# An attention and SoLU kernel: pair sums ahead of the block means, one transfer on another queue, and tiles at multiples of 512 bytes

## The chip, the cores and the metric

The kernel runs on one core of a Trainium2 chip. The metric is the device time of one execution in microseconds (us), the median over the runs shown; lower is better. The core's engines are TensorE (PE in the profile, with its weight loads as PEld), VectorE (DVE), ScalarE (ACT), GpSimd (POOL) and SyncE (SP, which here only issues transfers). Each has its own instruction stream and works through it in order; they wait for each other by semaphores. SBUF is the on-chip memory, 128 partitions wide; PSUM is where TensorE writes.

## The reference

Four batches of eight heads, 768 positions, head dimension 64. Each query sees the 31 keys around it and, besides, 24 summaries: every block of 32 keys is summarised by the maximum of its keys and by the mean of its values.

```python
k_sum = k.reshape(B, H, nb, block, D).max(axis=3)
v_sum = v.reshape(B, H, nb, block, D).mean(axis=3)      # the "means" below
scores_l = scale * np.matmul(q, k.transpose(0, 1, 3, 2))     # masked to |i - j| < 16
scores_s = scale * np.einsum('bhsd,bhnd->bhsn', q, k_sum) + np.log(block)
...
a = softmax over both together
x = np.matmul(a, np.concatenate([v, v_sum], axis=2))
...
h = x @ w_in                        # 512 -> 1024
solu = h * softmax(h)
ln = layernorm(solu) * g_ln
out = ln @ w_out                    # 1024 -> 512
```

`x` is rearranged to 3072 rows of 512 before `w_in`. Inputs and outputs are fp32.

## The kernel before

**Work and order.** The 3072 rows are 24 row blocks of 128 (t = 0 to 23). A group (b, g) is batch b and four windows of 64 queries (g = 0, 1, 2); it makes two row blocks. For each half of a group `scores` (line 578) forms the scores of four heads, VectorE adds the mask (597), ScalarE takes the exponentials (605), `values_turn` transposes them (633), and `values` (664, 672) multiplies with the values. The result goes to `xh` and `xl`, a rounded high part and the rest. `first(t)` (697) makes `h` from them in two halves of 512 columns; after the SoLU and its normalisation `turn(t)` transposes (633) into `lh` and `ll`, and `second(t)` (775) makes `o` and sends it out. Each product with `w_in` or `w_out` is three matmuls of 128 x 512 (high by low, low by high, high by high), the stationary operand a 128 x 128 piece of `xh`, `xl`, `lh` or `ll`, the moving one half of a `w` tile. So a row block of `h` is 2 x 4 x 3 = 24 matmuls, and one of `o` is 8 x 3 = 24 (the last is halved, 48 in two column halves).

**Weights.** `load_w` brings 16 raw tiles of 512 KB, and `rounded`, `split_w_in` and `split_w_out` turn each in place into a high and a low half, with some seven instructions on ScalarE and VectorE, sometimes GpSimd. These fill VectorE and ScalarE in the first 100 us.

**The means.** `vsum` is one tile, with the 24 means of a batch in partitions 96 to 119. For batch 0, `load_v_rows` (447) loads all values in three `st_v` tiles of two times 128 rows of 512 (each 512 KB), and `mean_values_first` (459) multiplies them with a selector: `sel` holds 1/32 where a row belongs to a block. That is six fp32 matmuls into one bank; the profile shows each as two entries. For batch 1 `mean_values_pe` (472) does it with another layout and selector (`sel_q`), and four small transfers on ScalarE's queue (485) put the rows into `vsum`. Batches 2 and 3 add on GpSimd (501) instead. `load_v2` (541) copies the means from `vsum` into the `vt` tile of a group, beneath its window values. For (0, 1) and (0, 2) this transfer is issued by ScalarE, for batches 1 to 3 by SyncE. Group (0, 0) has none: it multiplies with `vsum` directly (664).

**The planner.** The order of all engines is written out by a planner at build time. An `op` names the engines that can take it with a cost for each (`ADD_W = ((dve, 0.62), (pool, 1.46))`), the tiles it reads and writes, and from these its dependences. An operation's due time is the least position in the list among TensorE operations that need it. `order` simulates: each engine takes the ready operation that can begin first, then the one due first, but leaves an operation to another engine that would end it earlier. `issue` does that 64 times, 63 of them with noise on the due times, and keeps the order with the earliest planned end of TensorE. Where TensorE has to wait in the first 80 us, `keep_up` puts in fillers: bf16 matmuls of zeros (line 900), into a bank that is free.

**Where tiles lie.** A tile gets its address when it is first used, so small and large ones lie mixed. The `w` tiles follow `ident`, `mhalf`, `mask`, `g_sb` and `zero`. Of the tiles below, the remainder of the address by 512 is, in the program as built:

| tile | buffer 0 | buffer 1 | used by |
|---|---|---|---|
| all `w` tiles (4096 bytes) | 96 | | moving operand of 697 and 775 |
| `xh` and `xl` | 160 | 32 | 697; a group uses buffer (3b + g) mod 2 |
| `lh` | 160 | 352 | 775; buffer t mod 2 |
| `ll` | 352 | 96 | 775; buffer t mod 2 |

A 128 x 128 piece starts at a multiple of 512 bytes within its tile, a half of `w` at a multiple of 2048.

**Queues.** SyncE's order of first loads is the string `LOADS` (w for weights, k, q, r for `st_v`, v); its transfers share one queue. `load_v2` waits for the `load_v` of its group and for `vsum`; line 485 may write `vsum` only when every earlier `load_v2` has read it.

Of the kernel before, what the change touches and what calls it, by code (L numbers as in the profile page):

```python
# [11 lines left out]
F32 = mybir.dt.float32  # L12
F32R = mybir.dt.float32r
BF16 = mybir.dt.bfloat16
# [3 lines left out]
ALU = mybir.AluOpType  # L18
AX = mybir.AxisListType

P = 128
B, H, S, D = 4, 8, 768, 64
BLOCK, WINDOW = 32, 16
NB = S // BLOCK
DM, DF = H * D, 1024
# [7 lines left out]
WIN = QT + 2 * HALO  # L33
KC = WIN + NB
# [17 lines left out]
class Buf:  # L52


    def __init__(self, make, prev=()):
        self.make, self.prev, self.tile = make, prev, None
        self.ops, self.writers, self.readers, self.gone = [], {}, {}, False
# [15 lines left out]
class Plan:  # L73
# [14 lines left out]
    TRIES, NOISE = 64, 3.0  # L88

    def __init__(self):  # L90
        self.ops, self.rings, self.banks, self.idle = [], {}, {}, None

    def buf(self, pool, shape, dtype, tag, bufs, name):
        ring = self.rings.setdefault(tag, [])
        slot = f"{tag}_{len(ring) % bufs}"
        b = Buf(lambda: pool.tile(shape, dtype, tag=slot, bufs=1, name=name), ring[-bufs:][:1] if len(ring) >= bufs else ())
        ring.append(b)
        return b

    def place(self, make, bank, tag):  # L100

        b = Buf(make, [self.banks[bank]] if bank in self.banks else ())
        self.banks[bank] = b
        self.rings.setdefault(tag, []).append(b)
        return b

    def op(self, engine, cost, fn, r=(), w=(), nbytes=0, after=(), alt=(), port=False):

        deps = set(after)

        def of(table, part):
            for k, v in table.items():
                if part is None or k is None or k == part:
                    deps.update(v)

        o = Op({e: (c, f) for e, c, f in ((engine, cost, fn), *alt)}, deps,
               len(self.ops), nbytes, port)
        r = [x if isinstance(x, tuple) else (x, None) for x in r]  # L120
        w = [x if isinstance(x, tuple) else (x, None) for x in w]
        for b, part in r:
            of(b.writers, part)
        for b, part in w:
            of(b.writers, part)
            of(b.readers, part)
            for p in b.prev:
                deps.update(p.ops)
                p.gone = True
        assert not any(b.gone for b, _ in r + w)  # L130
        for b, part in r:
            b.readers.setdefault(part, []).append(o)
            b.ops.append(o)
        for b, part in w:
            b.writers.setdefault(part, []).append(o)
            b.ops.append(o)
        deps.discard(o)
        self.ops.append(o)
        return o
# [115 lines left out]
def attn_then_solu(ctx: ExitStack, tc: tile.TileContext, q, k, v, vr, vb, w_in, w_out, g_ln, out):  # L255
# [3 lines left out]
    nc = tc.nc  # L259
    plan = Plan()  # L260
    op = plan.op
    pe, act, dve, pool, sp = "pe", "act", "dve", "pool", "sp"
# [6 lines left out]
    COPY_X = ((act, 0.48), (dve, 0.6))  # L269
    LO_W = ((dve, 0.6), (pool, 1.4))  # L270
    ADD_W = ((dve, 0.62), (pool, 1.46))
    MUL_E = ((pool, 1.8), (dve, 1.07))

    const = ctx.enter_context(tc.tile_pool(name="const", bufs=1))
    sb = ctx.enter_context(tc.tile_pool(name="sb", bufs=1))
# [11 lines left out]
    def tt(costs, kind, to, a, b, **k):  # L287
        by = {dve: lambda: nc.vector.tensor_tensor(out=to(), in0=a(), in1=b(), op=kind),  # L288
              pool: lambda: nc.gpsimd.tensor_tensor(out=to(), in0=a(), in1=b(), op=kind)}
        one, *others = [(e, c, by[e]) for e, c in costs]  # L290
        op(*one, alt=others, **k)
# [4 lines left out]

    mask = const.tile([P, 3, KC], F32, name="mask")
    g_sb = const.tile([P, NFC], F32, name="g_sb")
    zero = const.tile([P, 512], BF16, name="zero")

    make_identity(nc, ident)
    nc.gpsimd.memset(mhalf, -0.5)
    nc.vector.memset(zero, 0.0)
    nc.gpsimd.memset(mask[:, :, :WIN], 0.0)
    nc.gpsimd.memset(mask[:, :, WIN:], math.log(BLOCK) / SCALE)
    for p0 in (0, QT):
# [3 lines left out]
            out=m, in_=m, pattern=[[0, 3], [1, WIN]], compare_op=ALU.is_ge, fill=NEG,  # L310
            base=-(HALO - WINDOW + 1), channel_multiplier=-1,
        )
        nc.gpsimd.affine_select(
            out=m, in_=m, pattern=[[0, 3], [-1, WIN]], compare_op=ALU.is_ge, fill=NEG,
            base=HALO + WINDOW - 1, channel_multiplier=1,
# [2 lines left out]
    nc.gpsimd.memset(mask[QT:, 2, HALO + QT:WIN], NEG)  # L318


    sel_b = plan.buf(sb, [P, S // P, NB], F32, "sel", 1, "sel")

    def selector():
        sel = sel_b.ap
        nc.gpsimd.memset(sel, 1.0 / BLOCK)
        nc.gpsimd.affine_select(
            out=sel, in_=sel, pattern=[[P, S // P], [-BLOCK, NB]], compare_op=ALU.is_ge, fill=0.0,
            base=0, channel_multiplier=1)
        nc.gpsimd.affine_select(
            out=sel, in_=sel, pattern=[[-P, S // P], [BLOCK, NB]], compare_op=ALU.is_ge, fill=0.0,  # L330
            base=BLOCK - 1, channel_multiplier=-1)

# [24 lines left out]
    def rounded(key, tag, bufs):  # L359
# [26 lines left out]

        tt(ADD_W, ALU.add, high, high, low, r=[(st, 1)], w=[(st, 0)], port=True)
        wt[key] = hl = plan.buf(const, [P, 2, 512], F32R, f"w{key}", 1, f"w{key}")
# [20 lines left out]
    def bank(i, tag, name):  # L409
        return plan.place(lambda: ps.tile([P, 512], F32, tag=f"bank{i}", bufs=1, name=name), i, tag)  # L410
# [38 lines left out]
    def mean_values_first(b):  # L449

        vsum[b] = y = plan.buf(sb, [P, DM], F32, "vsum", 1, f"vsum{b}")
        acc = bank(0, "h", f"vs_ps{b}")
        n = S // P
        for i in range(n // 2):
            x = vst[b, i]

            def mm(i=i, x=x):
                for c in (2 * i, 2 * i + 1):
                    nc.tensor.matmul(  # L459
                        acc.ap[WIN:KC, :DM], sel_b.ap[:, c, :], x.ap[:, c % 2, :],  # L460
                        start=(c == 0), stop=(c == n - 1))
            op(pe, 1.7, mm, r=[x, sel_b], w=[acc])
        op(act, 0.48, lambda: nc.scalar.copy(out=y.ap[WIN:KC, :], in_=acc.ap[WIN:KC, :DM]), r=[acc], w=[y])

    def mean_values_pe(b):
# [71 lines left out]

    def load_v2(b, g):
        x, y = vt[b, g], vsum[b]
        e, cost, queue = (sp, 0.43, nc.sync) if b else (act, 0.8, nc.scalar)  # L540
        return op(e, cost, lambda: queue.dma_start(
            out=x.ap[WIN:KC], in_=y.ap[WIN:KC, :].rearrange("p (o c) -> p o c", o=1).broadcast_to([NB, G, DM])),
            r=[y], w=[(x, 1)], nbytes=NB * 8192)

    def scores(b, g, pp, direct=False, each=False):
# [62 lines left out]
        for i in range(2):  # L608
            op(act, 1.52, lambda i=i: exps(i), r=[nm], w=[(e, i), (z, i)])
        op(act, 0.2, lambda: nc.scalar.activation(out=z.ap, in_=z.ap, func=AF.Copy, bias=1e-9), w=[z])  # L610
        op(dve, 0.1, lambda: nc.vector.reciprocal(out=z.ap, in_=z.ap), w=[z])
        tt(MUL_E, ALU.mult, lambda: e.ap, lambda: e.ap,
           lambda: z.ap.rearrange("p (u o) -> p u o", o=1).broadcast_to([P, 8, KC]), r=[z], w=[e], port=True)
# [188 lines left out]
    for pp in range(NPP):  # L802
        for p in (2 * pp, 2 * pp + 1):
            key_blocks(0, p)
        run(scores(0, 0, pp, True, True))
        if pp == 0:
            op(pool, 0.8, selector, w=[sel_b])
            mean_values_first(0)
    for i in range(2 * NKC):
        split_w_in(*divmod(i, 2))  # L810
        if i % 2 == 0 and i < 2 * NPP:
            run(values_turn(0, 0, i // 2))
            run(values(0, 0, i // 2, 0, True))

    begun = [load_v2(*its[1])]
    for i in range(3):
        load_v_rows(1, i)
# [3 lines left out]
    rows = [(hh, i) for hh in range(2) for i in range(2)]  # L821
# [16 lines left out]
    for t in range(NT):  # L838
        n, j = divmod(t, 2)
        b, g = its[n]  # L840
# [47 lines left out]
        if j == 1 and n + 2 < len(its):  # L888
            load_v2(*its[n + 2])
# [10 lines left out]
        nc.tensor.matmul(x[:, :n], zero[:, :P], zero[:, :n], start=True, stop=True)  # L900

    plan.idle = idle
    plan.issue()


# [38 lines left out]
```

## Time and profile before

| | us |
|---|---|
| runs | 396.39, 397.99, 946.64 |
| median | 397.99 |
| the profiled execution | 397.45 |
| its span, first to last instruction | 395.7 |
| granted TensorE clock | 0.999 of full |

The 946.64 is a single outlier. Durations are read from the profiled execution. Busy time is what an engine's instructions took; TensorE's holds the fillers too. A group row of the profile gives line, engine, operation, the tile written and the tiles read, the shape, the count, then busy time and mean duration. In the chain of waits every piece is the work, or the wait, that the next had to wait for. In the timeline a row has start, length, engine, line, tiles and the number of instructions merged in it; SPq and ACTq rows are transfers being issued, not moved.

### The profile page before, as it was taken

The page shows a single profiled execution, that of the slowest core. Times are in us where ns is not written, and L with a number is a line of the kernel's source. Part 1 is how long each engine was busy: PE and PEld are TensorE (multiplying, and loading weights), DVE is VectorE, ACT ScalarE, POOL GpSimd, SP SyncE. Part 2 cuts the span into 40 slices and gives each one's busy share as a digit, 9 for nine tenths or more (in the row PEclk, how much of TensorE's full clock was granted, in tenths as well). Part 3 has the DMA queues.
Part 4 walks back from the last instruction along what each step waited for, and adds up shares of the span by engine and source line. Part 5 has one row for each costly group of instructions (what it writes and reads, how often), then busy time and mean ns, then how long its engine had stood idle before and what let it go on. Part 6 is the DMA issues. An engine that isn't in the chain of part 4 may idle for free.

```text
span 395.7 us, 9677 instructions
## 1 busy us (share of the span) xinstructions
PE 386.6 (98%) x3697; PEld 298.3 (75%) x3703; DVE 275.4 (70%) x884; ACT 248.7 (63%) x746; POOL 97.9 (25%) x245
## 2 busy tenths in 40 slices
PE   8999998999999999999999999999999999999996
PEld 3436766677878888878888888878888887878776
DVE  4999998999789866577767657657657654554330
ACT  3889686999798756658558466468466463533411
POOL 4224010416837221236220121221021021101100
PEclk9999999999999999999999999999999999999999
DMA  7999992136277320463330410430310000000011
GB/s 287 411 410 369 409 329 78 56 113 185 70 248 208 113 103 0 141 175 104 123 112 2 150 66 27 156 73 28 108 48 27 2 28 27 16 12 28 27 55 53
DMA packets 14994, 49.24 MB, mean 124 GB/s; under 512 B 1836, under 2 KB 2092, under 8 KB 13412
## 3 DMA queue, kind: packets, MB, share of 16 engines
q1 hardware_dynamic: 11084, 41.89, 30.8%
q10 hardware_dynamic: 3864, 6.74, 4.7%
q8 instruction: 29, 0.48, 0.5%
q14 instruction: 17, 0.14, 0.1%
HBM read 40.11 MB, written 6.29 MB: 117 GB/s over the span
## 4 chain that ended last, share of the span: by engine, by line
PE 85%; DMA 6%; ACT 3%; DVE 2%; issue 1%; ACTq 1%; SPq 1%; DVEq 0%
PE o L775 35%; PE h L697 30%; PE x L672 6%; PE s L578 5%; PE t L633 3%; PE lt L633 3%; DMA st_v<-in_vr 3%; DMA raw<-in_w_in 2%; DMA vt<-vsum 2%; PE vs_ps L459 1%; PE x L900 1%; ACT he L712 1%; DVE he L720 1%; ACT at L281 1%; PE x L664 1%
## 5 line engine op out<-in xcount | busy, mean ns | idle before, releaser
L775 PE MATMUL o<-w,lh 128*128 128x512 f32 (+1 forms) x400 | 128.0, 390 | 0.1
L697 PE MATMUL h<-w,xh 128*128 128x512 f32 x384 | 127.0, 398 | 0.4 <-DVE he L720 0.4
L605 ACT ACTIVATE e<-e,nm 128x120 f32<-128x120 f32 x192 | 73.1, 385 | 25.0 <-DVE nm L597 25.0
L775 PEld LDWEIGHTS o<-w,lh 128*128 128x128 f32 x400 | 74.1, 188 | 18.5 <-issue 2.4
L697 PEld LDWEIGHTS h<-w,xh 128*128 128x128 f32 x384 | 72.1, 188 | 18.9 <-ACT e L605 0.8
L775 PE MATMUL o<-w,ll 128*128 128x512 f32 (+1 forms) x200 | 76.9, 384 | 0.0
L697 PE MATMUL h<-w,xl 128*128 128x512 f32 x192 | 75.6, 394 | 0.0
L707 DVE TENSOR_REDUCE hm<-h 128x1 f32<-128x512 f32 x48 | 32.6, 686 | 42.7 <-PE h L697 42.7
L281 ACT COPY at<-t 120x512 f32<-120x512 f32 x46 | 24.8, 587 | 46.1 <-PE t L633 45.6
L775 PEld LDWEIGHTS o<-w,ll 128*128 128x128 f32 x200 | 37.6, 188 | 6.6
L697 PEld LDWEIGHTS h<-w,xl 128*128 128x128 f32 x192 | 36.1, 188 | 7.5
L597 DVE CUSTOM_DVE_ANT_0 e<-s,mask 128x120 f32<-128x120 f32 x192 | 40.6, 276 | 1.3 <-PE s L578 1.3
L712 ACT ACTIVATE he<-h,hm 128x512 f32<-128x512 f32 x48 | 32.8, 697 | 9.4 <-DVE hm L709 9.4
L605 ACT ACTIVATION_READ_ACCUMULATOR e<-e,nm 128x1 f32 x192 | 36.5, 190 | 0.0
L760 DVE TENSOR_TENSOR ll<-lt,lh 128x512 fp32r<-128x512 f32 x48 | 31.9, 682 | 6.0 <-ACT lh L281 5.8
L739 POOL TENSOR_SCALAR ss<-ss 128x1 f32<-128x1 f32 x24 | 7.1, 297 | 115.0 <-ACT sq L735 114.9
L720 DVE SCALAR_TENSOR_TENSOR he<-h,hz,he 128x512 f32<-128x512 f32 x48 | 34.1, 746 | 0.4
L672 PE MATMUL x<-at,vt 120*64 120x64 f32 (+1 forms) x768 | 28.3, 225 | 1.5 <-ACT at L281 1.5
L672 PEld LDWEIGHTS x<-at,vt 120*64 120x64 f32 (+1 forms) x768 | 24.6, 138 | 6.3 <-ACT at L281 2.8
L288 DVE TENSOR_TENSOR e<-e,z 128x960 f32<-128x960 f32 x23 | 26.6, 1156 | 0.5
L281 ACT CAST lh<-lt 128x512 fp32r<-128x512 f32 x33 | 18.6, 596 | 12.9 <-PE lt L633 10.0
L735 ACT ACTIVATE sq<-he 128x1024 bf16<-128x1024 f32 x24 | 25.2, 1050 | 0.2
(94 smaller groups left out, 499.6 us busy)
## 6 DMA issues: line engine op xcount, KB each, us to landing
vt<-in_v SPq DMA_DIRECT2D x12, 1024.0 KB, 5.4
kraw<-in_k SPq DMA_DIRECT2D x16, 400.0 KB, 9.1
out<-os ACTq DMA_DIRECT2D x23, 256.0 KB, 2.0
qt<-in_q SPq DMA_DIRECT2D x11, 512.0 KB, 5.5
raw<-in_w_in SPq DMA_DIRECT2D x8, 512.0 KB, 10.7
raw<-in_w_out SPq DMA_DIRECT2D x8, 512.0 KB, 9.5
st_v<-in_vr SPq DMA_DIRECT2D x6, 512.0 KB, 12.5
st_v<-in_vb SPq DMA_DIRECT2D x8, 384.0 KB, 3.3
```

Of the source, the lines that this page charges most:

```text
L281: by = {act: lambda: nc.scalar.copy(out=to(), in_=of()), dve: lambda: nc.vector.tensor_copy(out=to(), in_=of()), pool: lambda: nc.gpsimd.t ...
L288: by = {dve: lambda: nc.vector.tensor_tensor(out=to(), in0=a(), in1=b(), op=kind), pool: lambda: nc.gpsimd.tensor_tensor(out=to(), in0=a() ...
L597: nc.vector.tensor_tensor_reduce(out=e.ap[:, n, :], in0=sc.ap[:, j, (2 * i + up) * KC:(2 * i + up + 1) * KC], in1=mask[:, mi, :], scale=-S ...
L605: nc.scalar.activation(out=e.ap[:, n, :], in_=e.ap[:, n, :], func=AF.Exp, bias=nm.ap[:, n:n + 1], scale=-1.0, accum_out=z.ap[:, n:n + 1])
L672: nc.tensor.matmul(xp()[j * D:(j + 1) * D, i, qs], vs.ap[:k, u, cs], at.ap[:k, u % 2, n[j] + u // 2, :], start=not apart, stop=not apart o ...
L697: nc.tensor.matmul(hp.ap, a.ap[:, c, ts], w.ap[:, i], start=(c == 0 and n == 0), stop=(c == NKC - 1 and n == 2))
L707: op(dve, 0.6, lambda i=i, hp=hp: nc.vector.tensor_reduce(out=nms.ap[:, i:i + 1], in_=hp.ap, op=ALU.max, axis=AX.X, negate=True), r=[hp], ...
L712: op(act, 0.71, lambda i=i, hp=hp: nc.scalar.activation(out=part(i), in_=hp.ap, func=AF.Exp, bias=nm.ap, accum_out=zs.ap[:, i:i + 1]), r=[ ...
L720: op(dve, 0.67, lambda i=i, hp=hp: nc.vector.scalar_tensor_tensor(out=part(i), in0=hp.ap, scalar=zs.ap[:, 0:1], in1=part(i), op0=ALU.mult, ...
L735: op(act, 1.13, lambda: nc.scalar.activation(out=sq.ap, in_=e.ap, func=AF.Square, accum_out=ss.ap), r=[e], w=[sq, ss])
L760: op(dve, 0.6, lambda part=part, r=r: nc.vector.tensor_tensor(out=part(lo), in0=tp.ap[:, r], in1=part(hi).bitcast(F32), op=ALU.subtract), ...
L775: nc.tensor.matmul(o.ap[:, cols], a.ap[:, f, :], w.ap[:, i, cols], start=(f == 0 and n == 0), stop=(f == NFC - 1 and n == 2))
```

## The change

Three edits in one.

1. *Pair sums.* The host lays the rows of batch 0 so that a partition holds two neighbouring keys. One addition per `st_v` tile (cost 1.46 on GpSimd or 0.62 on VectorE) adds the two, and one matmul in place of two sums the blocks. The selector has three pieces in place of six, with blocks of 16 pairs.
2. *The third group's means.* `load_v2` of (0, 2) is issued by SyncE instead of ScalarE.
3. *Layout.* `lay_out`, called before the program is issued, asks for the address of every tile's slot in order of the size's largest power of two (up to 2048): first the tiles whose size is a multiple of 2048, then the rest. `zero` grows from 1024 to 1952 bytes, of which the same 1024 are used. With the 128 bytes before them the constants then end at 128 + 512 + 32 + 1440 + 32 + 1952 = 4096, so `w`, `xh`, `xl`, `lh`, `ll`, `vt`, `qt`, `at`, `he` and the other tiles of 2048, 4096 and 8192 bytes lie at multiples of 512. `kraw` (6400 bytes), `kw` and `e` (3840) lie at multiples of 256; `ident` and `mask` stay where they were.

```diff
+        if len(ring) < bufs:
+            self.slots.append((tag, math.prod(shape[1:]) * (2 if dtype == BF16 else 4), b))
...
+    def lay_out(self):
+        for _, _, b in sorted(self.slots, key=lambda x: -math.gcd(x[1], 2048)):
+            b.ap
...
+    ADD_V = ((pool, 1.46), (dve, 0.62))
...
-    zero = const.tile([P, 512], BF16, name="zero")
+    zero = const.tile([P, 976], BF16, name="zero")
...
-    nc.vector.memset(zero, 0.0)
+    nc.vector.memset(zero[:, :512], 0.0)
...
-    sel_b = plan.buf(sb, [P, S // P, NB], F32, "sel", 1, "sel")
+    sel_b = plan.buf(sb, [P, S // P // 2, NB], F32, "sel", 1, "sel")
...
-            out=sel, in_=sel, pattern=[[P, S // P], [-BLOCK, NB]], compare_op=ALU.is_ge, fill=0.0,
+            out=sel, in_=sel, pattern=[[P, S // P // 2], [-BLOCK // 2, NB]], compare_op=ALU.is_ge, fill=0.0,
...
-        n = S // P
-        for i in range(n // 2):
+        n = S // P // 2
+        for i in range(n):
             x = vst[b, i]
-
-            def mm(i=i, x=x):
-                for c in (2 * i, 2 * i + 1):
-                    nc.tensor.matmul(
-                        acc.ap[WIN:KC, :DM], sel_b.ap[:, c, :], x.ap[:, c % 2, :],
-                        start=(c == 0), stop=(c == n - 1))
-            op(pe, 1.7, mm, r=[x, sel_b], w=[acc])
+            tt(ADD_V, ALU.add, lambda x=x: x.ap[:, 0], lambda x=x: x.ap[:, 0], lambda x=x: x.ap[:, 1],
+               w=[x], port=True)
+            op(pe, 0.85, lambda i=i, x=x: nc.tensor.matmul(
+                acc.ap[WIN:KC, :DM], sel_b.ap[:, i, :], x.ap[:, 0, :], start=i == 0, stop=i == n - 1),
+               r=[x, sel_b], w=[acc])
...
-        e, cost, queue = (sp, 0.43, nc.sync) if b else (act, 0.8, nc.scalar)
+        e, cost, queue = (sp, 0.43, nc.sync) if b or g > 1 else (act, 0.8, nc.scalar)
...
+    plan.lay_out()
     plan.issue()
...
-        "vr": np.ascontiguousarray(np.stack([rows[0], rows[1, keys]]).reshape(2, 3, 2, P, DM).transpose(0, 1, 3, 2, 4)),
+        "vr": np.ascontiguousarray(np.stack([
+            rows[0].reshape(3, P, 2, DM), rows[1, keys].reshape(3, 2, P, DM).transpose(0, 2, 1, 3)])),
```

More of the change, by code (lines that the diff above doesn't have):

```diff
@@ L90, in __init__ @@
     def __init__(self):
-        self.ops, self.rings, self.banks, self.idle = [], {}, {}, None
+        self.ops, self.rings, self.banks, self.idle, self.slots = [], {}, {}, None, []
     def buf(self, pool, shape, dtype, tag, bufs, name):
@@ L326, in selector @@
         nc.gpsimd.affine_select(
-            out=sel, in_=sel, pattern=[[P, S // P], [-BLOCK, NB]], compare_op=ALU.is_ge, fill=0.0,
+            out=sel, in_=sel, pattern=[[P, S // P // 2], [-BLOCK // 2, NB]], compare_op=ALU.is_ge, fill=0.0,
             base=0, channel_multiplier=1)
         nc.gpsimd.affine_select(
-            out=sel, in_=sel, pattern=[[-P, S // P], [BLOCK, NB]], compare_op=ALU.is_ge, fill=0.0,
-            base=BLOCK - 1, channel_multiplier=-1)
+            out=sel, in_=sel, pattern=[[-P, S // P // 2], [BLOCK // 2, NB]], compare_op=ALU.is_ge, fill=0.0,
+            base=BLOCK // 2 - 1, channel_multiplier=-1)
     sel_q = plan.buf(sb, [P, 3, 32], F32, "sel", 1, "sel_q")
```

## The prediction

> **What bounds the kernel now.** I read the page first, then the table of busy time by window, then the chain of waits in order of time, then the timeline of the first 70 us and of two stretches in the middle.
>
> ```profile
> span 395.7 us, 9677 instructions
> PE 386.6 (98%) x3697; PEld 298.3 (75%) x3703; DVE 275.4 (70%) x884; ACT 248.7 (63%) x746; POOL 97.9 (25%) x245
> ...
> PE 85%; DMA 6%; ACT 3%; DVE 2%; issue 1%; ACTq 1%; SPq 1%; DVEq 0%
> ...
> L775 PE MATMUL o<-w,lh 128*128 128x512 f32 (+1 forms) x400 | 128.0, 390 | 0.1
> L697 PE MATMUL h<-w,xh 128*128 128x512 f32 x384 | 127.0, 398 | 0.4 <-DVE he L720 0.4
> ```
>
> ```profile
> 20.00:30.00 10.00, 9.32 (x71) 3.46 (x72) 9.96 (x30) 8.31 (x28) 1.77 (x2) 1.00 1.02 410
> 30.00:40.00 10.00, 9.84 (x142) 6.35 (x143) 9.92 (x33) 9.53 (x38) 4.81 (x13) 1.00 1.03 368
> ...
> 60.00:70.00 10.00, 8.99 (x120) 6.77 (x118) 8.27 (x19) 6.74 (x14) 1.21 (x3) 1.00 0.25 66
> 70.00:80.00 10.00, 9.14 (x78) 6.27 (x77) 10.00 (x48) 10.00 (x36) 4.39 (x14) 1.00 0.13 48
> ...
> 90.00:100.00 10.00, 9.34 (x120) 7.20 (x119) 9.81 (x35) 9.70 (x32) 7.09 (x13) 1.00 0.54 155
> 100.00:200.00 100.00, 99.94 (x1040) 81.08 (x1039) 75.02 (x259) 67.53 (x212) 39.34 (x90) 1.00 0.41 133
> 200.00:300.00 100.00, 100.00 (x1016) 81.65 (x1014) 65.64 (x230) 63.07 (x207) 19.02 (x53) 1.00 0.22 70
> ```
>
> In a window row the columns are length, PE, PEld, DVE, ACT, POOL (each with its count), granted clock, DMA share and GB/s. There are two regimes. From 100 us on TensorE is never idle (99.94 and 100.00 of 100 us) at a full clock, while VectorE stands at 75 and 66%: there the time is the number of matmuls by the spacing of their starts, and what shortens that spacing shortens the run one for one. Before 100 us VectorE is full (9.96, 9.92, 10.00, 9.81 of 10), and TensorE's busy time holds fillers (line 900). Work taken off TensorE there counts only as far as VectorE and ScalarE follow.
>
> The chain gives the spacing: 24 matmuls make one row block of `h` (line 697) or `o` (line 775).
>
> ```profile
> 38.39 5.79 PE h L697 x24
> ...
> 135.81 5.66 PE o L775 x24
> 141.47 5.60 PE h L697 x24
> ...
> 150.25 5.75 PE o L775 x24
> ...
> 186.22 5.49 PE h L697 x24
> ```
>
> The same 24 matmuls on the same `w` tiles take 5.60 us, 233.3 ns each, in the block at 141 us (t = 8, which reads buffer 0 of `xh` and `xl`) and 5.49 us, 228.8 ns each, at 186 us (t = 11, buffer 1). `o` takes 5.66 us from buffer 1 of `lh`/`ll` (t = 3) and 5.75 us from buffer 0 (t = 4). What differs between the buffers is where they lie: 160 bytes past a multiple of 512 for `xh`/`xl` 0, 32 for `xh`/`xl` 1; 160 and 352 for `lh`/`ll` 0; 352 and 96 for `lh`/`ll` 1. The moving `w` tiles all lie at 96. So **the address of a tile seems to be worth nanoseconds on the bounding engine**, and the third part of the change, which looks like housekeeping, touches all 1176 of these matmuls.
>
> **The layout.** An `o` block begins with two long gaps after a change of shape, so the spacing inside it is read from every third start:
>
> ```profile
> 138.14 0.39 PE L775 MATMUL o<-w,ll 128*128 128x512 f32 x1
> ...
> 138.82 0.39 PE L775 MATMUL o<-w,ll 128*128 128x512 f32 x1
> ...
> 152.61 0.39 PE L775 MATMUL o<-w,ll 128*128 128x512 f32 x1
> ...
> 154.69 0.39 PE L775 MATMUL o<-w,ll 128*128 128x512 f32 x1
> ```
>
> 0.68 us for three is 226.7 ns from buffer 1; 2.08 us for nine is 231.1 ns from buffer 0. After the change `w`, `xh`, `xl`, `lh` and `ll` all lie at a multiple of 512. No row of before shows that case. The nearest is `lh`/`ll` 1, the only pair where stationary and moving operand have one remainder by 256 (96), as all will: 226.7 ns, which I take. Then `h` gains 288 x (233.3 - 226.7) = 1.9 us on buffer 0 and 288 x (228.8 - 226.7) = 0.6 us on buffer 1, and `o` 288 x 4.4 ns = 1.3 us on buffer 0: 3.8 us. Five of the 24 `h` blocks run before 100 us, where I count half: **3.5 us**.
>
> The bounds. On the fast side stands a matmul of the same shape in bf16, the filler:
>
> ```profile
> L900 PE MATMUL vs_ps<-zero x50: 379/379/635, 1.2 to 19.2; 128*128 128x512 bf16 x50
> ...
> 17.09 2.54 PE L900 MATMUL vs_ps<-zero 128*128 128x512 bf16 x11 [0.16 <-issue]
> ```
>
> Eleven in 2.54 us, the last of them 0.38 us long: (2.54 - 0.38) / 10 = 216 ns. At that spacing `h` gains 576 x 15 ns = 8.6 us and `o` 288 x 15.1 and 264 x 10.7 ns = 7.2 us: 15.8 us. On the slow side every block runs like `xh` 0, at 233.3 ns: 288 x 4.5 ns for `h`, 288 x 2.2 and 264 x 6.6 ns for `o`, a loss of 3.6 us.
>
> Loads land in the moved tiles too, at 410 GB/s with a DMA share of 1.02, saturated. I take 0 for it; half a microsecond either way of the 12.5 us that a `vr` load takes (row below) is the widest I allow.
>
> **The pair sums.**
>
> ```profile
> L459 PE MATMUL vs_ps<-st_v,sel x12: 590/592/609, 20.5 to 29.8; 128*24 128x512 f32 x12
> ...
> st_v<-in_vr SPq DMA_DIRECT2D x6, 512.0 KB, 12.5
> ...
> 11.12 0.69 DVE L379 SCALAR_TENSOR_TENSOR cv<-cv 128x512 int32<-128x512 int32 x1
> ...
> 14.16 0.33 SPq L447 DMA_DIRECT2D st_v<-in_vr  x1
> ...
> 20.05 1.71 POOL L289 TENSOR_TENSOR cv<-cv 128x512 int32<-128x512 int32 x1
> 20.57 1.75 DVE L379 SCALAR_TENSOR_TENSOR cv<-cv 128x512 int32<-128x512 int32 x1
> ...
> 26.74 3.61 PE L459 MATMUL vs_ps<-st_v,sel 128*24 128x512 f32 x8
> ...
> 27.24 0.68 DVE L288 TENSOR_TENSOR w<-cv,w 128x512 fp32r<-128x512 f32 x1
> ...
> 30.28 0.68 PE L633 MATMUL t<-ident,e 64*120 64x64 f32 x16
> ```
>
> Each program matmul of line 459 is two entries: twelve before, four at 20.5 and eight at 26.74 us, (3.61 - 0.59) / 7 = 0.43 us apart. After there are six. The third `vr` tile is issued at 14.16 and lands 12.5 us later, at 26.66 us, 0.08 us before TensorE starts the eight. Until then TensorE waits in fillers, so what the first tile's entries save is worth nothing. After: the second tile's pair can run in filler time; the third needs one add (0.68 us by the row at 27.24), two more handovers of 0.08 us, then 2 x 0.43 us: done at 28.4 instead of 30.3 us, **1.9 us earlier**; 1.0 us if the planner leaves both tiles until the last has landed.
>
> Against it stand three adds on a full VectorE, 3 x 0.68 = 2.0 us. The planner may give them to GpSimd (it books 1.46 us there against 0.62), but that holds VectorE up as well: the L379 instruction that started inside GpSimd's 1.71 us took 1.75 us, against 0.69 at 11.12; three such are 3.2 us. The Trainium skill, page "SBUF — State Buffer", section "Who interferes with whom", has this as a rule: a VectorE instruction with two SBUF inputs contends with a GpSimd one that reads SBUF. The trace agrees with the 1.75 us; by the rule the adds are no free work for GpSimd, and it speaks against the change.
>
> VectorE idles 1.73 us in 60 to 70, and in that window and the next TensorE waits for it and for ScalarE (8.99 and 9.14 us busy). So most of the 1.9 us should come back as such waits: I take a net **0.5 us**. The ends are a gain of 1.9 us and, with the adds on GpSimd and the early start lost, a loss of 3.2 - 1.73 = 1.5 us. The selector's own work is hidden by GpSimd's idleness (1.77 us busy of 10) and by the wait for the first tile; halved, it can't cost more than now.
>
> **The means' transfer.** One DMA, `load_v2` of batch 0, group 2, moves from ScalarE's queue to SyncE's.
>
> ```profile
> 53.50 6.18 DMA vt<-vsum
> 59.69 1.35 issue
> 61.04 0.72 ACTq L485
> ...
> 65.41 0.95 ACT at L281 x2
> ```
>
> ```profile
> 43.82 5.20 SPq L430 DMA_DIRECT2D kraw<-in_k  x4
> 53.50 0.81 ACTq L541 DMA_DIRECT2D vt<-vsum  x1
> 55.48 0.33 SPq L535 DMA_DIRECT2D vt<-in_v  x1
> ```
>
> Its issue of 0.81 us lies beside a copy that ScalarE is running. But the transfer reads `vsum`, which line 485 overwrites, so ScalarE stands 1.35 us from 59.69 until it is over; behind that wait are the `kw` copy, a `w` piece and the `at` copy at 65.41 for which TensorE then waits. On SyncE the issue falls between the last `kraw` load (49.0) and the `vt` load at 55.48; it can land microseconds sooner, or, queued behind `kraw`, no sooner. Behind it SyncE holds only that `vt` load, used blocks later. Gain 0 to 1.35 us; if it lands later than now, ScalarE waits as much longer, 1 us at most by the room before 55.48. I take **0.5 us**.
>
> **The planner** draws its order anew, since its noise goes by the position in the list of operations. I price that at 0, with 1.3 us either way: half of TensorE's idle time in the three early windows (1.01, 0.86, 0.66 us).
>
> Sum: 3.5 + 0.5 + 0.5 = 4.5 us. The profiled execution took 397.45 us around its span of 395.7, close to the median of 397.99; so 397.45 - 4.5 = **393.0 us**.
>
> **The rivals.** *The spacing falls below every row of before*, towards the filler's 216 ns. For it: the array passes 512 columns in that time, and the blocks' spacing moves with the buffers alone. Against: the fillers are bf16, and no fp32 block comes near. At its end 397.45 - 15.8 - 1.0 = 380.7 us; half way, 388.5.
>
> *The layout costs time* (the other side): at multiples of 512 the stationary load meets the moving stream as badly as `xh` 0 does now, 233.3 ns in all blocks. For it: 32 and 160 are both worse than 96, and nothing says on which side 0 falls. It decides as soon as the mean spacing exceeds the present 230.1 ns. 397.45 + 3.6 - 1.0 = 400.1 us.
>
> *The layout is worth nothing and VectorE takes the early gain*: the blocks differ by something that goes with the buffers but not with their addresses, and VectorE is 2.0 us later less the 1.73 us it idles. For it: VectorE's full windows. 397.45 + 0.3 = 397.8 us. The section named above also says that TensorE waits on nobody for SBUF; by it the layout is worth 0, and 5.60 against 5.49 us do not agree with it.
>
> **How the numbers follow.** Forecast (fastest row's pace) 0.45, lower spacing 0.25, no effect 0.18, dearer layout 0.12. The forecast's own range is 390 to 395.5 us. The range for 8 in 10 reaches into the cases on both sides: 382 to 399.5 us. A change under 2%, 8 us, can't be told from none here. Faster by more needs a mean spacing under some 224 ns, which is most of the second case and a little of the first: 0.27. Slower by more needs the dearer layout and all the bad ends beside it: 0.03. The rest, 0.70, is within 2%.
>
> **What would show it.** Right: in the chain after 100 us every block of 24 takes alike whatever the buffer, 5.44 us for `h` and 5.66 for `o`; L459 has six entries; the first `h` block starts one to two microseconds before 38.39 us; line 541 has one issue on ScalarE. Wrong: blocks still differ by buffer (then addresses were not the cause), or `h` blocks sit near 5.2 us (lower spacing) or all at 5.6 (dearer layout), or TensorE's idle time from 60 to 100 us grows by more than 2 us (VectorE took more than I gave it).

## The result and the profile after

| | before | after |
|---|---|---|
| median of seven runs (us) | 396.96 | 394.72 |
| the profiled execution (us) | 397.45 | 394.53 |
| its span (us) | 395.7 | 392.8 |

The ratio after to before is 0.9949 [0.9931, 0.9967]: 2.0 us less by the ratio, 2.2 us by the medians, where 4.5 us were predicted, and 394.72 us in place of the 393.0 forecast. It is a gain under 2%, inside the predicted range. Two disturbed executions, 946.64 us of the kernel before and 1115.32 us of the pair-sum kernel below, stand in the medians but in no ratio. The text below takes apart why the gain is half of what was forecast: one term of the sum came out larger, one came out at nothing, and two turned into losses.

The page of the kernel after (its line numbers are those of before plus 8 or 9: 697 is now 705, 775 is 783, 541 is 549, and 459 is 468):

```profile
span 392.8 us, 9684 instructions
PE 382.1 (97%) x3699; PEld 297.5 (76%) x3704; DVE 276.2 (70%) x883; ACT 249.0 (63%) x746; POOL 102.7 (26%) x249
...
PE 74%; DVE 13%; ACT 7%; DMA 2%; issue 1%; SPq 1%; ACTq 1%
...
L705 PE MATMUL h<-w,xh 128*128 128x512 f32 x384 | 126.2, 394 | 1.9 <-DVE he L728 1.9
L783 PE MATMUL o<-w,lh 128*128 128x512 f32 (+1 forms) x400 | 127.7, 388 | 0.0
```

TensorE is busy 4.5 us less (386.6 to 382.1), the predicted 4.5 us by chance. The span fell by 2.9 us only: TensorE now idles more. The chain's shares say the same: VectorE holds 13% of it in place of 2%, ScalarE 7% in place of 3%.

The chain of waits after 130 us:

```profile
135.57 1.05 PE s L586 x32
...
141.61 5.44 PE h L705 x24
...
150.23 5.66 PE o L783 x24
155.89 5.44 PE h L705 x24
...
164.50 5.66 PE o L783 x24
...
199.96 5.44 PE h L705 x24
```

The blocks of `h` take 5.44 us and those of `o` 5.66, whatever the buffer; before, the blocks at the same places took 5.60 or 5.49 and 5.75 or 5.66. (Two `h` blocks, those that follow the means' matmuls of batches 2 and 3, begin with the long gaps of a change of shape: 5.66 us, before 5.70 and 5.79.) But the block of t = 8 begins at 141.61, where it began at 141.47: at that point the kernel had gained nothing. From there to the end of the span it takes 251.2 us in place of 254.2. So all of the gain is behind t = 8, and the windows show what happens ahead of it (columns as in the prediction; the first row is of the kernel before, the others of the kernel after):

```profile
40.00:50.00 10.00, 10.00 (x83) 7.78 (x83) 9.42 (x21) 6.14 (x16) 0.00 (x0) 1.00 1.04 412
...
40.00:50.00 10.00, 9.11 (x105) 5.95 (x103) 9.93 (x38) 9.01 (x35) 1.71 (x2) 1.00 0.97 366
...
60.00:70.00 10.00, 8.93 (x121) 6.96 (x119) 8.89 (x20) 7.72 (x17) 4.48 (x8) 1.00 0.24 64
...
100.00:200.00 100.00, 98.39 (x1036) 80.26 (x1035) 74.83 (x260) 69.88 (x224) 40.30 (x95) 1.00 0.41 137
200.00:300.00 100.00, 100.00 (x1020) 82.58 (x1019) 66.56 (x232) 60.54 (x198) 19.67 (x54) 1.00 0.21 70
```

TensorE idles 0.89 us in 40 to 50 (before: 0.00) and 1.61 us in 100 to 200 (before: 0.06). The second regime, in which TensorE sets the time alone, begins only at 135.57 us, where the chain leaves VectorE and ScalarE until its last piece; in the kernel before it began at 96.19. TensorE's timeline shows the order that the planner drew:

```profile
33.44 0.50 PE L705 MATMUL h<-w,xh 128*128 128x512 f32 x1
...
43.04 1.90 PE L908 MATMUL x<-zero 128*128 128x512 bf16 x7
45.73 0.69 PE L641 MATMUL t<-ident,e 64*120 64x64 f32 x16 [0.79 <-DVE hz L723]
46.35 0.82 PE L908 MATMUL x<-zero 128*128 128x512 bf16 x3
...
69.92 0.50 PE L705 MATMUL h<-w,xh 128*128 128x512 f32 x1 [1.07 <-DVE he L728]
```

The first `h` block begins at 33.44, 5 us earlier than before, since SyncE issues the first `st_v` load at 3.78 us in place of 9.56. Behind it stand fillers (line 908) and waits for VectorE, and at t = 8 the 5 us are gone.

### The profile page after: what moved, and what is told of

It reads as the page before. It is cut to its first block, busy times and chain, and to the rows that moved or that the text cites. A ratio compares the mean times of both kernels' runs of the same rounds, so it can differ in the third digit from the quotient of the medians.

```text
span 392.8 us, 9684 instructions
## 1 busy us (share of the span) xinstructions
PE 382.1 (97%) x3699; PEld 297.5 (76%) x3704; DVE 276.2 (70%) x883; ACT 249.0 (63%) x746; POOL 102.7 (26%) x249
## 4 chain that ended last, share of the span: by engine, by line
PE 74%; DVE 13%; ACT 7%; DMA 2%; issue 1%; SPq 1%; ACTq 1%
PE o L783 32%; PE h L705 27%; PE x L680 5%; PE s L586 4%; PE lt L641 3%; PE t L641 3%; DVE e L605 2%; DMA st_v<-in_vr 2%; ACT e L613 2%; ACT he L720 1%; DVE e L297 1%; DVE cv L389 1%; DVE ll L768 1%; ACT at L290 1%; DVE hm L715 1%
## 5 line engine op out<-in xcount | busy, mean ns | idle before, releaser
L705 PE MATMUL h<-w,xl 128*128 128x512 f32 x192 | 74.8, 390 | 0.0
L736 POOL TENSOR_SCALAR he<-he,nmu 128x512 f32<-128x512 f32 x13 | 13.7, 1054 | 71.4 <-DVE nmu L731 71.4
L747 POOL TENSOR_SCALAR ss<-ss 128x1 f32<-128x1 f32 x24 | 6.1, 252 | 94.9 <-ACT sq L743 94.9
```

The lines of the kernel that those rows point to most:

```text
L705: nc.tensor.matmul(hp.ap, a.ap[:, c, ts], w.ap[:, i], start=(c == 0 and n == 0), stop=(c == NKC - 1 and n == 2))
```

## The experiments

The change's three edits alter the planner's order in two ways: by what they cost, and by shifting the noise, which goes by the position in the list. So the edits were tried alone with the order held, and the order alone with the edits held. "Draw 8" is the draw whose order the kernel before runs. The ratios are to the kernel before, on the same chip; their intervals are worth some 0.3 to 0.7 us either way, so a difference of a few tenths between two rows is not resolved.

| kernel | median (us) | ratio |
|---|---|---|
| layout alone | 392.43 | 0.9885 [0.987, 0.9901] |
| the change without its layout | 400.22 | 1.0082 [1.0064, 1.01] |
| layout and pair sums, draw held | 393.42 | 0.9908 [0.989, 0.9925] |
| the same once more | 393.56 | 0.9915 [0.9899, 0.993] |
| layout and transfer, draw held | 396.34 | 0.9987 [0.9975, 0.9999] |
| layout, every tile at 160 | 394.93 | 0.9943 [0.9927, 0.996] |
| layout, `w` at 0, the others at 64 | 398.16 | 1.0032 [1.0016, 1.0048] |
| layout, `w` at 0, the others at 32 | 399.0 | 1.005 [1.0037, 1.0064] |
| layout and transfer, order kept | 392.48 | 0.989 [0.9875, 0.9905] |
| layout, second-best draw | 396.4 | 0.9992 [0.9976, 1.0008] |
| before and transfer, order kept | 396.75 | 0.999 [0.9981, 0.9998] |
| layout, pair sums, transfer, order held | 393.32 | 0.9908 [0.9894, 0.9921] |

**The layout alone.** `lay_out` and the longer `zero` put on the kernel before; every engine's order stays as it was.

```diff
-    zero = const.tile([P, 512], BF16, name="zero")
+    zero = const.tile([P, 976], BF16, name="zero")
...
+    plan.lay_out()
     plan.issue()
```

> Before with the layout edit alone; the order of all engines is that of before, instruction for instruction. Theory (the layout is worth 3 us or more, since TensorE has no idle time after 100 us, and the two other edits with their new order give some of it back): all blocks of 24 at 226.7 ns, 5.44 us for h; 393.0 to 393.5 us, 3.5 to 4 us under before and 1 to 1.5 us under the whole change. Rival (the layout is worth only the 2.2 us that the whole change brings, the early edits nothing): 394.7 us, level with the whole change.

It took 392.43 us, 4.6 us under before by the ratio, and so less time than the whole change. Its chain:

```profile
54.01 5.20 DMA vt<-vsum
...
59.31 0.69 ACTq L491
...
139.31 5.44 PE h L703 x24
...
147.93 5.66 PE o L781 x24
153.59 5.44 PE h L703 x24
```

From the block at 139.31 to the end of its span of 390.7 us are 251.4 us, 2.8 less than before. The prediction's spacings give 2.7 us there: of the 16 `h` blocks from t = 8 on, 24 x 8 x 6.6 ns and 24 x 8 x 2.1 ns, and of some 20 `o` blocks 24 x 10 x 4.4 ns. The other 1.8 us were won ahead of t = 8 (2.2 us between the two profiled executions). There ScalarE's wait behind the means' transfer is gone: by the chain the transfer is over by 59.21, and ScalarE goes on at 59.31 (before: 61.04, with 1.35 us of waiting). The chain names no releaser for those 1.35 us; that they belong to the transfer follows from the program, and from a run below that moves nothing but this transfer.

**The change without its layout.** The opposite edit, on the kernel after: `lay_out` out and `zero` short. In that build `w` lies at 96 again, but `xh` and `xl` at 480 and 416, and `lh` and `ll` at other remainders than in the kernel before.

```diff
-    plan.lay_out()
     plan.issue()
```

> The changed kernel without the layout edit: pair sums, moved transfer and the new order of the whole change, kept instruction for instruction. The stationary tiles then lie at 480 and 416 (xh, xl), 224 and 480 (lh) and w at 96. Theory: the early edits give nothing or lose, 397 to 398.5 us, not below before, although h starts near 33 us as in the whole change. Rival (early start helps, layout less): below 396 us.

It took 400.22 us, 5.3 us more than the change by the two ratios. Its chain:

```profile
143.67 5.57 PE h L705 x24
...
152.42 5.77 PE o L783 x24
```

232 ns for `h` and 240 ns with the long gaps for `o`, against 226.7 and 236 of the kernel after, which is 0.12 us for each of 48 blocks, 5.8 us, less what lies in the first 100 us. By 256 the `xh` and `xl` of the block at 143.67 lie 128 from `w`. Without the layout the rest of the change is a loss of 0.8%.

**Pair sums and layout, the draw held.** The adds take no noise, so that the other operations keep theirs, and the planner is given draw 8 alone.

```diff
-        for seed in range(self.TRIES):
+        for seed in (8,):
...
-                o.due = x + (noise.gauss(0.0, self.NOISE) if seed else 0.0)
+                o.due = x + (noise.gauss(0.0, self.NOISE) if seed and not o.quiet else 0.0)
...
+            plan.ops[-1].quiet = True
```

> The layout kernel with the pair sums added, and the planner held to the draw of before (one seed; the three new additions take no noise), so that the order of loads is that of before and TensorE's nearly. Theory (TensorE's saving of 1 to 2 us at 30 us is eaten by 2 us more on a full VectorE): within 0.8 us of the layout kernel, either way. Rival (the prediction's net gain): 0.5 us or more below it; second rival (additions cost VectorE more than they save): 1.5 us above it.

The median is 393.42 us, a loss of 1.0 us to the layout alone. The same kernel ran a second time, and its trace is the one read here:

> The layout kernel with the pair sums in the held draw once more, for a profile. Theory: 393.4 us, 1.0 us above the layout kernel, as VectorE takes the additions and its order before 40 us is late by them; h starts earlier all the same. Rival: level with the layout kernel within 0.3 us.

It took 393.56 us, 1.1 us over the layout alone. First the tile view of `st_v` in this kernel (durations in ns are least, median, greatest, then the first and the last start):

```profile
L295 DVE TENSOR_TENSOR st_v<-st_v x3: 679/680/1569, 20.7 to 27.7; 128x512 f32<-128x512 f32 x3
```

then its timeline:

```profile
20.05 1.72 POOL L296 TENSOR_TENSOR cv<-cv 128x512 int32<-128x512 int32 x1
20.74 2.17 DVE L295 TENSOR_TENSOR st_v<-st_v 128x512 f32<-128x512 f32 x2
...
27.65 0.68 DVE L295 TENSOR_TENSOR st_v<-st_v 128x512 f32<-128x512 f32 x1
28.60 1.90 PE L466 MATMUL vs_ps<-st_v,sel 128*24 128x512 f32 x4
...
34.03 2.97 PE L906 MATMUL h<-zero 128*128 128x512 bf16 x13 [0.16 <-issue]
39.32 0.50 PE L703 MATMUL h<-w,xh 128*128 128x512 f32 x1
```

and that of the layout alone:

```profile
26.36 3.61 PE L465 MATMUL vs_ps<-st_v,sel 128*24 128x512 f32 x8
...
34.12 1.46 PE L906 MATMUL h<-zero 128*128 128x512 bf16 x6 [0.16 <-issue]
38.05 0.50 PE L703 MATMUL h<-w,xh 128*128 128x512 f32 x1
```

All three adds went to VectorE. The first began while GpSimd held its 1.72 us instruction and took 1.57 us; the third waited its turn among VectorE's other work and began at 27.65. So the means were summed at 30.50, where eight entries without adds ended at 29.97: 0.5 us later and not earlier. VectorE's other results slid with them, the filler ahead of the last `x` products doubled (2.97 for 1.46 us), and the first `h` block began 1.27 us later. The loss in the whole time is 1.1 us; TensorE's shorter work was paid with fillers.

**Transfer and layout, the draw held.**

```diff
-        e, cost, queue = (sp, 0.43, nc.sync) if b else (act, 0.8, nc.scalar)
+        e, cost, queue = (sp, 0.43, nc.sync) if b or g > 1 else (act, 0.8, nc.scalar)
...
-        for seed in range(self.TRIES):
+        for seed in (8,):
```

> The layout kernel with only the transfer of the third group's means moved to SyncE's queue, planner held to the draw of before. Theory (ScalarE's 1.35 us wait before the four small transfers goes, but TensorE's wait after it is filled by other waits): 0 to 0.5 us below the layout kernel. Rival (it lands later on SyncE's queue, and ScalarE waits longer): 0.5 to 1 us above it.

It took 396.34 us, 3.9 us more than the layout alone. Its chain and, behind it, TensorE's timeline:

```profile
62.72 1.15 ACT sq L741 x2
...
64.39 1.33 ACT he L738 x2
65.72 0.94 ACT at L287 x2
```

```profile
66.71 1.15 PE L678 MATMUL x<-at,vt 120*64 120x64 f32 x32 [0.82 <-ACT at L287]
...
70.76 0.50 PE L703 MATMUL h<-w,xh 128*128 128x512 f32 x1 [1.27 <-DVE he L726]
...
93.04 0.69 PE L639 MATMUL t<-ident,e 64*120 64x64 f32 x16 [1.55 <-DVE e L294]
```

The planner booked 0.8 us less on ScalarE and moved other work into the room: `sq` and `he` now stand ahead of the `at` copies, which begin 2.07 us later than with the layout alone (65.72 for 63.65), and TensorE waits at three places, 3.64 us in all (its idle time from 60 to 100 us is 3.76 us, with the layout alone 1.25). That is a cost of the new order. To see the transfer itself, it was issued by SyncE while the planner went on booking it on ScalarE, so that every order stays:

```diff
-        e, cost, queue = (sp, 0.43, nc.sync) if b else (act, 0.8, nc.scalar)
+        e, cost, queue = (sp, 0.43, nc.sync) if b else (act, 0.8, nc.sync if g > 1 else nc.scalar)
```

On the layout:

> The layout kernel with the third group's means issued by SyncE while the planner still books them on ScalarE, so that every engine keeps its order and only the one transfer changes its queue. Theory (the 3.9 us that the moved transfer cost came from the new order around it, not from the transfer): 391.9 to 392.9 us. Rival (the transfer itself comes late on SyncE's queue or holds up loads behind it): 394.5 us or more.

It took 392.48 us, the same as the layout alone (392.43): 0.0 us by the medians, 0.2 us more by the ratios. On the kernel before, with its old layout:

> Before, tiles where they were, with the third group's means issued by SyncE and every engine's order kept as in before. In the old layout ScalarE stood 1.35 us behind this transfer. Theory (the wait goes with the queue, and most of it reaches TensorE's wait behind it): 0.5 to 1.3 us below before, 396.0 to 396.7 us beside 397.2. Rival (the transfer lands no sooner on SyncE's queue): 397.0 to 397.5 us.

It took 396.75 us beside 397.31: a ratio of 0.999 [0.9981, 0.9998], a gain of 0.4 us by the ratio and 0.6 by the medians. Its chain, where the same place has 1.35 us before:

```profile
54.28 5.47 DMA vt<-vsum
59.75 0.47 issue
60.22 0.71 ACTq L485
```

Only the transfer's queue differs, and ScalarE's wait falls to 0.47 us. The transfer is worth some half a microsecond, just clear of the noise, where ScalarE waits for it, and nothing that can be resolved where the layout has already ended that wait.

**What in the address counts.** Three kernels move tiles by a constant. `zero` grown to 1056 elements puts `w` and the stationary tiles alike at 160:

```diff
-    zero = const.tile([P, 976], BF16, name="zero")
+    zero = const.tile([P, 1056], BF16, name="zero")
```

> The layout kernel with every laid-out tile shifted by 160 bytes: w, xh, xl, lh and ll all lie 160 past a multiple of 512, the address at which xh 0 was slowest before (233.3 ns). Theory (what counts is the distance of the stationary tile from the moving one, which is 0): 226.7 ns, 392.4 us as the layout kernel. Rival (what counts is the stationary tile's own remainder): 233 ns in all blocks, 1128 x 6.7 ns = 7.5 us more, about 400 us.

A pad behind `w` leaves `w` at 0 and puts the stationary tiles at 64, or at 32 with 8 elements:

```diff
     plan.lay_out()
+    const.tile([P, 16], F32, name="pad")
```

> The layout kernel with 64 bytes between the w tiles and all others: w stays at multiples of 512, the stationary tiles lie 64 past one, as far from w as xh 0 lay before (160 against 96). Theory (distance counts): 233.4 ns, about 399.5 us. Rival (the stationary tile's own remainder counts, and any multiple of 64 is as good as 512): 226.7 ns, 392.4 us.

> The layout kernel with 32 bytes between the w tiles and the others: a distance not yet measured. Theory (distance 0 by 256 is the best, others lie between 229 and 233 ns): 395 to 398 us, spacing above 228 ns. Rival (only the 64-byte line counts, 32 is as good as 0 or better): 226.7 ns or less, 392.5 us or less.

The chains, first with all at 160, then with 64 between, then with 32 between:

```profile
60.04 2.17 issue
...
142.16 5.44 PE h L703 x24
...
150.78 5.67 PE o L781 x24
156.45 5.44 PE h L703 x24
```

```profile
140.69 5.60 PE h L703 x24
...
149.46 5.79 PE o L781 x24
```

```profile
141.03 5.60 PE h L703 x24
...
149.80 5.80 PE o L781 x24
```

At 160 the blocks are as quick as at 0. At a distance of 64 or 32 they are slow, 233.3 ns for `h`, in every block and both buffers. So what counts is the distance between the stationary and the moving tile, and not where either lies. It is to be taken by 256: in the kernel before, `lh` of buffer 1 lay at 352 by 512, 256 bytes further than `w` at 96, and `ll` of buffer 1 lay at 96, and their blocks had the 226.7 ns. The shift to 160 nevertheless cost 2.5 us to the layout alone, all of it ahead of t = 8 (142.16 for 139.31): there ScalarE's wait behind the transfer is back, at 2.17 us. Why the transfer comes later is not settled. The loads hint at it: their mean rate from 20 to 30 us was 409 GB/s here and 410 in each of the three kernels with `w` at 96 (the kernel before, the same with its transfer moved, the change without its layout), while the nine with `w` at 0 gave 413 to 420 (415 and 413 with the other tiles at 64 and 32). One profile of each shows no overlap, but not that this rate is what ends the wait: at 64 and 32 a wait of 0.29 and 0.68 us was left.

**The draw.** The layout alone, with the planner held to its second-best draw, whose planned end is 0.25 us behind that of draw 8:

```diff
-        for seed in range(self.TRIES):
+        for seed in (42,):
```

> The layout kernel in the planner's second-best draw, whose planned end is 0.25 us after the best; nothing else differs. Theory (draws that the planner holds equal differ by 1 to 4 us on the chip, since VectorE's and ScalarE's order before 100 us decides): 393.5 to 396.5 us. Rival (the draws are worth what the planner says): 392.7 us.

It took 396.4 us: 4.0 us more for a plan that is 0.25 us worse, with the same operations, of which some run on another engine, and other fillers. One of its waits, from the timeline:

```profile
68.58 0.34 PE L678 MATMUL x<-at,vt 120*64 120x64 f32 x4 [0.74 <-ACT at L287]
```

Its `h` block of t = 8 begins 2.75 us later than with draw 8 (141.90 for 139.15 in the timelines). The last kernel has the layout, the pair sums with the draw held, and the transfer with its order kept, so the whole change but its new draw:

> All three edits with the planner held: layout, pair sums in the held draw, the transfer on SyncE's queue but booked on ScalarE. Theory (the edits add up once the order is held: 392.4 + 1.0 + 0.0): 393.4 us, 1.3 us below the change as it stands, which is what its new draw costs. Rival (the loss is in the edits together): 394.5 us or more.

It took 393.32 us, a ratio of 0.9908 [0.9894, 0.9921] where the change as made has 0.9949 [0.9931, 0.9967]. So the change's own new draw costs 0.0041 x 397 = 1.6 us by the ratios, 1.4 by the medians, though its planned end was 1.1 us earlier than that of the kernel before.

With these the sum closes: -4.6 (layout) + 1.1 (pair sums) + 0.0 (transfer) + 1.6 (new draw) = -1.9 us, measured -2.0. Since the last term is itself the remainder between the change and the last kernel, what this tests is the first three: they make -3.5 us, and the last kernel shows -3.7. The best version is the layout alone, 392.43 us: 2.3 us below the change.

**Where the early time is decided.** In the kernels that keep the order of draw 8, the block of t = 8 follows one event at a fixed distance: the first of the four small transfers of line 485 (491 with the layout), the one that waits for the means' transfer. Its start is read from the timelines, that of the block from the chains.

| kernel | first small transfer (us) | `h` of t = 8 (us) | between |
|---|---|---|---|
| before | 61.04 | 141.47 | 80.43 |
| before and transfer, order kept | 60.22 | 140.62 | 80.40 |
| layout alone | 59.28 | 139.31 | 80.03 |
| layout and transfer, order kept | 59.51 | 139.48 | 79.97 |
| layout and pair sums, draw held | 60.41 | 140.40 | 79.99 |
| layout, every tile at 160 | 62.21 | 142.16 | 79.95 |
| layout, the others at 64 | 60.02 | 140.69 | 80.67 |
| layout, the others at 32 | 60.36 | 141.03 | 80.67 |

The event moves by 2.9 us from kernel to kernel, and the distance behind it goes with the spacing alone. So of the 2.2 us that the layout won ahead of t = 8 in its profile, 0.4 us lie behind the event, as spacing, and 1.8 us ahead of it: 1.35 us are the wait, the rest ScalarE's earlier arrival. The losses by the pair sums (1.1 us) and by the shift to 160 (2.9 us in its profile) pass through the same event.

## Why the prediction was half right

The total lies within the forecast's own range of 390 to 395.5 us, but partly by luck: the layout brought 1.1 us more than its 3.5, the pair sums missed their term by 1.6 us the other way, the transfer by 0.5, and the draw added 1.6.

**Right: the spacing.** The forecast that all blocks come to the 226.7 ns of "the only pair where stationary and moving operand have one remainder by 256" was right to the digit: 5.44 and 5.66 us, and the kernels with a distance of 32 or 64 and with all tiles at 160 exclude that the absolute address or the buffer is the cause. The rivals on the spacing fall with the rows above: no block came below 5.44 (the lower spacing), none stayed at 5.6 (the dearer layout), and the layout was worth 4.6 us and not nothing. (The other half of that third rival, VectorE taking the early gain, is what the pair sums show.) Behind t = 8 the term was right in size: 2.7 us by the spacings, 2.8 us measured.

The prediction named as a rule against this that TensorE waits on nobody for SBUF. It is from the Trainium skill, page "SBUF — State Buffer", section "Who interferes with whom", whose table also says that TensorE's two read ports, for the moving operand and the weights, are independent, and that it shares them with no one. The 5.60 and 5.44 us blocks with one instruction stream and two distances do not agree with that for these matmuls. What in the chip the distance decides was not found out.

**Mis-sized: the loads in the moved tiles.** The step "I take 0 for it" with half a microsecond either way failed. Ahead of t = 8 the layout alone won 1.8 us, where the halved spacing of five `h` blocks and the early `o` blocks account for 0.7. The rest, 1.1 us, goes with the end of ScalarE's 1.35 us wait behind the means' transfer. The prediction had the row of that wait before it, and gave all of it to the transfer's own edit. That the wait ended is shown; that the loads' new addresses ended it is likely by their rates, and not shown.

**So the transfer came out at 0.** Taken alone the step was right: 0.5 us predicted, 0.4 to 0.6 measured in the old layout. In the sum it was counted on a wait that another edit of the same change takes away, and there it is worth nothing that these runs resolve.

**Wrong in sign: the pair sums.** The failing step is "done at 28.4 instead of 30.3 us, 1.9 us earlier". It let the third add begin as its tile landed, at 26.66; the add began at 27.65, behind VectorE's other work, and the second pair's matmul too ran only after it. The means came 0.5 us later. With no early gain left, the price that the prediction did name (three adds on a full VectorE) stood alone: a loss of 1.1 us, inside its ends of a gain of 1.9 and a loss of 1.5. The rule that the prediction quoted there from the Trainium skill, page "SBUF — State Buffer", section "Who interferes with whom", has a VectorE instruction with two SBUF inputs contend with a GpSimd one that reads SBUF. The trace agrees with it: the first add took 1.57 us beside GpSimd's 1.72, and the others 0.68.

**Mis-sized: the new draw.** "I price that at 0, with 1.3 us either way" took the bound from TensorE's idle time in three windows. The change's draw cost 1.4 to 1.6 us, another draw of the layout kernel 4.0, and the new order around the moved transfer 3.9. A draw also moves fillers, which count as busy, and work on VectorE and ScalarE, which the idle time of TensorE does not bound.

Of what should have shown the steps right, the first block's early start did come, but at 33.44 and not one to two microseconds before 38.39; with the order held it came 1 us later instead (39.32). It was the draw's doing, and no sign that the pair sums pay. TensorE's idle time from 60 to 100 us fell (2.53 to 1.59 us), so the sign for "VectorE took more than I gave it" stood in the wrong windows: the idle time grew at 40 to 50 and behind 100. The six entries of line 459 (now 468) and the single issue of line 541 (now 549) on ScalarE came as forecast.

## What to carry to other kernels

When blocks of identical matmuls differ by buffer, compare the addresses of their stationary and moving tiles: here giving both one remainder by 256 bytes was worth 1.2% for an edit of a few lines, some 0.9% of it by the spacing itself. When a heuristic orders the program, a changed list of operations is a new order, worth up to 4 us of 397 here; hold the order to judge an edit, and try several orders on the chip, since the planned end was no guide between them: a plan 0.25 us worse cost 4.0 us, and one 1.1 us better lost 1.4 to 1.6. Two edits that remove the same wait are paid for it once.

## What the runs showed of the hardware

A matmul of 128 x 512 on fp32r tiles (fp32 values that the kernel has rounded) with a 128 x 128 stationary operand is spaced 226.7 ns when stationary and moving tile lie at the same remainder by 256 bytes (all at 0, all at 160), and 233.3 ns when the stationary tile lies 32 or 64 bytes further. At 192 further, in the kernel before, it was 228.8 ns, and at 128 further, in the change without its layout, 232 ns. The remainder itself changes nothing in the spacing. A matmul with nothing to wait for can thus lose 3% to the place of its operands.
